# Score units of 384 or 512 columns per head in place of 384, and six larger buffers for exponentials, in the first attention batch of a fused attention and expert kernel

## The chip, the cores and the metric

The kernel runs on one core of one Trainium2 chip. The metric is the device time of the core in microseconds (us). The kernel before takes 275.0 us (median of 6 runs, 274.83 to 275.27).

A run is called fast unless it is over 1.5% above the fastest run of the same kernel. All comparisons below are of fast runs. "Clock" is the mean clock that the throttle granted to TensorE in a run, as a share of full speed.

## The reference

Block-sparse causal attention for 4 batches of 8 heads, 768 tokens and 64 columns, then a two-layer expert with a Gelu between.

```python
# attention, for each batch and head (S = 768, blocks of 64 keys)
gate   = q @ mean of k over each block        # causal blocks only
top    = the three best blocks of a query     # and the query's own block
scores = q @ k.T / 8, where the block is chosen and the key is not later
attn   = softmax(scores);  x = attn @ v       # x: 3072 x 512

# expert
h   = x @ w_in                                # 3072 x 2048
g   = 0.5 * h * (1 + tanh(sqrt(2/pi) * (h + 0.044715 * h**3)))
out = g @ w_out                               # 3072 x 512
```

## The kernel before

Two heads are handled as a pair; a batch has four pairs (0 to 3, 4 to 7, ...). A batch is: for each pair load, transpose, gate, mask, scores, exponentials, values, normalise; then the dense expert of the batch (`s1` is x times w_in with the Gelu, `s2` is the product with w_out).

The kernel does not emit its work in source order. Every piece of work is an operation with an assumed duration on each engine that may do it. A small list scheduler in the kernel, "the planner" below, simulates the engines and gives one total order. Each engine then runs its part of it in that order, and waits wherever data are late.

```python
LAT = {"PE": 0.2, "ACT": 0.19, "DVE": 0.14, "POOL": 0.1, "SP": 0.1,
       "DMA": 1.9, "XBAR": 0.1, "NONE": 0.0}     # from the end of a work to its users
...
    def solve(self):
        while cand:
            ...                                  # all ready operations and engines
            s, end, e, op = min(
                (x for x in ests if x[0] <= first),
                key=lambda x: (x[3].prio, x[3].n, x[1]))
            ...
        order.sort(key=lambda op: op.start)
        return order
...
    order = plan.solve()
    with tc.manual_schedule():
        for op in order:
            op.emit(op.eng)
```

The first batch computes both heads of a pair in one score unit. A unit is a list of pieces (key tile of 128, first query, number of queries); its scores fill at most 2 x 512 columns of a PSUM pair of banks (`wide`), and one exponential reads them:

```python
units = [[(0, 0, 384)], [(1, 128, 256), (2, 256, 128)], [(0, 384, 384)],
         [(1, 384, 384)], [(2, 384, 384)], [(3, 384, 384)],
         [(4, 512, 256), (5, 640, 128)]]          # seven units of 384 per head

st = add({PE: 0.45}, st_e, rdy[p][0 if ui < 2 else 1], pr, ...)   # scores and mask
ex = add({ACT: 0.71}, ex_e, [st, table(("exp", b), [], base)], pr, ...)
...                                               # af: causal edge on POOL
pvs.append(add({PE: 0.212}, pv_e, [af, ...], pr, ...))            # values
nm = add({DVE: 0.7}, zr_e, pvs[-1:], base - 20, ...)              # norm: reciprocal, multiply
```

TensorE's gaps are filled with 110 dummy matmuls, "fillers", at the lowest priority. What is left of them runs at the very end:

```python
def warm():
    for n in range(110):
        ...                    # nc.tensor.matmul(bank[:, 0:256], zero, zero...)
        add({PE: 0.107 if n > 26 else 0.214}, emit, [], 1e6, ...)
```

The softmax here doesn't subtract the row's maximum and nothing guards it: scores larger than these inputs give would overflow.

Of the kernel before, what the change touches and what calls it, by code (L numbers as in the profile page):

```python
# [9 lines left out]
FP16 = mybir.dt.float16  # L10
# [23 lines left out]
class Plan:  # L34
# [13 lines left out]
    def add(self, *a, **kw):  # L48
        op = Op(*a, **kw)
        self.ops.append(op)  # L50
        return op
# [70 lines left out]
def kernel(  # L122
# [28 lines left out]
    iov = ctx.enter_context(tc.tile_pool(name="iov", bufs=PV))  # L151
    hd = ctx.enter_context(tc.tile_pool(name="hd", bufs=3))
    hd2 = ctx.enter_context(tc.tile_pool(name="hd2", bufs=2))
    atp = ctx.enter_context(tc.tile_pool(name="atp", bufs=7))
    xtp = ctx.enter_context(tc.tile_pool(name="xtp", bufs=2))
    gtp = ctx.enter_context(tc.tile_pool(name="gtp", bufs=2))
    obp = ctx.enter_context(tc.tile_pool(name="obp", bufs=3))
# [35 lines left out]
    PE, ACT, DVE, POOL, SP = "PE", "ACT", "DVE", "POOL", "SP"  # L193
    add = plan.add
    T = {}
# [171 lines left out]
    rdy = {}  # L367
# [381 lines left out]
    def heads(p):  # L749
        b, hp = divmod(p, HP)  # L750
        i = p % NB
        base = 1000 * b + 100 * hp
        norms = []
        for h in range(2):
            pvs = []
            for gi, (ja, jb) in enumerate(groups):
                u = (p, h, gi)
                pr = base + 10 * (3 * h + gi)
                wa = S - ja * 128
                wb = S - jb * 128  # L760

                def st_e(_, u=u, ja=ja, jb=jb, wa=wa, wb=wb, h=h):
                    st = plan.buf[("st",) + u]
                    for jc, cb in ((ja, 0), (jb, wa)):
                        s0 = jc * 128
                        w = S - s0
                        x = cb
                        while x < cb + w:
                            e = min(cb + w, (x // 512 + 1) * 512)
                            k0, q0 = slice(s0, s0 + 128), slice(  # L770
                                s0 + (x - cb), s0 + (e - cb))
                            nc.tensor.matmul(  # L772
                                st[:, x:e], kT16[i][h][0:76, k0],
                                qT16[i][h][0:76, q0],
                                start=True, stop=True)
                            x = e
                st = add({PE: 0.381}, st_e, rdy[p][h], pr,
                         takes=("wide", ("st",) + u))

                def ex_e(_, u=u, n=wa + wb):  # L780
                    T["at", u] = atp.tile([128, 896], FP16, tag="at",
                                          name="at_%d_%d_%d" % u)
                    nc.scalar.activation(
                        out=T["at", u][:, 0:n],
                        in_=plan.buf[("st",) + u][:, 0:n],
                        func=AF.Exp, bias=0.0, scale=SCALE)
                ex = add({ACT: 0.8}, ex_e,
                         [st, table(("exp", b), gelus.get(b - 1, []), base)],
                         pr,
                         gives=[("st",) + u])  # L790
                exps.setdefault(b, []).append(ex)

                def af_e(_, u=u, wa=wa):
                    at = T["at", u]
                    dg = bass.AP(at.tensor, at.offset,
                                 [at.ap[0], [wa, 2], [1, 128]])
                    nc.gpsimd.affine_select(
                        out=dg, in_=dg, compare_op=ALU.is_ge, fill=0.0,
                        base=0, pattern=[[0, 2], [1, 128]],
                        channel_multiplier=-1)  # L800
                af = add({POOL: 0.36}, af_e, [ex], pr)

                def pv_e(_, u=u, ja=ja, jb=jb, wa=wa, h=h, gi=gi):
                    pvv = plan.buf["pv", p, h][:, 0:NC * 66].rearrange(
                        "p (c w) -> p c w", w=66)
                    at = T["at", u]
                    for jc, cb in ((ja, 0), (jb, wa)):
                        for qc in range(jc, NC):
                            nc.tensor.matmul(
                                pvv[:, qc, 0:65],  # L810
                                at[:, cb + (qc - jc) * 128:
                                   cb + (qc - jc + 1) * 128],
                                v16[i][:, jc, h, :],
                                start=(gi == 0 and jc == 0 and qc == 0),
                                stop=(gi == 2 and jc == jb and qc == NC - 1),
                                skip_group_check=True)
                pvs.append(add({PE: 0.212}, pv_e,
                               [af, ld["v16", p], c_E["ones", i]] + pvs[-1:],
                               pr, takes=("pv", ("pv", p, h))))

            norms.append(norm(p, h, pvs, base - 20))
        turn(p, norms)
        last.setdefault(p, {}).update({"s": st, "k": st, "v": pvs[-1]})


    units = [[(0, 0, 384)], [(1, 128, 256), (2, 256, 128)], [(0, 384, 384)],
             [(1, 384, 384)], [(2, 384, 384)], [(3, 384, 384)],
             [(4, 512, 256), (5, 640, 128)]]

    def both_heads(p):  # L830

# [4 lines left out]
        pvs = []  # L836
        for ui, pieces in enumerate(units):
            u = (p, ui)
            pr = base + 10 * ui

            def st_e(_, u=u, pieces=pieces):

                st = plan.buf[("st",) + u]
                for mask in range(2):
                    x = 0
                    for j, q0, w in pieces:
# [8 lines left out]
                                start=x == 0 and not mask, stop=bool(mask),  # L855
                                skip_group_check=True)
                        x += w
            st = add({PE: 0.45}, st_e, rdy[p][0 if ui < 2 else 1], pr,
                     takes=("wide", ("st",) + u))

            def both(t, lo, hi):
                return t[:, 0:768].rearrange("p (h w) -> p h w", h=2)[
                    :, :, lo:hi]

            def ex_e(_, u=u):
                T["at", u] = atp.tile([128, 896], FP16, tag="at",
                                      name="at_%d_%d" % u)
                nc.scalar.activation(
                    out=both(T["at", u], 0, 384),
                    in_=plan.buf[("st",) + u].rearrange(  # L870
                        "p (h w) -> p h w", h=2)[:, :, 0:384],
                    func=AF.Exp, bias=0.0, scale=SCALE)
            ex = add({ACT: 0.71}, ex_e,
                     [st, table(("exp", b), [], base)], pr,
                     gives=[("st",) + u])
            exps.setdefault(b, []).append(ex)
            af = ex
            for n, (j, q0, w) in enumerate(pieces):
                if q0 != 128 * j:
                    continue  # L880
                x = sum(w for _, _, w in pieces[:n])

                def af_e(_, u=u, x=x):
                    dg = both(T["at", u], x, x + 128)
                    nc.gpsimd.affine_select(
                        out=dg, in_=dg, compare_op=ALU.is_ge, fill=0.0,
                        base=0, pattern=[[0, 2], [1, 128]],
                        channel_multiplier=-1)
                af = add({POOL: 0.36}, af_e, [ex], pr)

            half = 0 if ui < 2 else 1

            def pv_e(_, u=u, ui=ui, pieces=pieces, half=half):
                pvv = plan.buf["pv", p, half][:, 0:NC * 66].rearrange(
                    "p (h c w) -> p h c w", h=2, w=66)
                x = 0
                for j, q0, w in pieces:
                    for c in range(q0 // 128, (q0 + w) // 128):
                        for h in range(2):
                            nc.tensor.matmul(  # L900
                                pvv[:, h, c - 3 * half, 0:65],
                                both(T["at", u], x, x + 128)[:, h],
                                v16[i][:, j, h, :],
                                start=(ui in (0, 2) and x == 0 and h == 0),
                                stop=(ui in (1, len(units) - 1)
                                      and x == 256 and h == 1),
                                skip_group_check=True)
                        x += 128
            pvs.append(add({PE: 0.212}, pv_e,
                           [af, ld["v16", p], c_E["ones", i]] + pvs[-1:],  # L910
                           pr, takes=("pv", ("pv", p, half))))
            if ui == 1 or ui == len(units) - 1:
# [252 lines left out]
```

## Time and profile before

| stage, us from the start of the span | TensorE busy | VectorE | ScalarE | clock |
|---|---|---|---|---|
| 28 to 36 (first batch, pairs 2 and 3) | 8.00 of 8 | 7.83 | 7.32 | 1.00 |
| 36 to 44 (first batch, pair 3) | 7.87 of 8 | 6.63 | 6.77 | 1.00 |
| 48 to 67 (dense expert, first batch) | 19.00 of 19 | 5.86 | 13.11 | 1.00 |
| 160 to 193 (end of the second batch's `s2`, then the third batch's `s1`) | 33.00 of 33 | 11.77 | 18.98 | 1.00 |

The names of the engines in the profile: PE is TensorE, DVE is VectorE, ACT is ScalarE, SP issues the loads. These are lines of the page of the kernel before: the span, the busy times, and the granted clock in 40 slices of the span (9 is 90% or more).

```profile
span 273.8 us, 5919 instructions
PE 265.1 (97%) x2290; PEld 153.7 (56%) x2290; DVE 142.2 (52%) x468; ACT 187.4 (68%) x245; POOL 48.5 (18%) x112
PEclk9999999999999999999999999999999999999999
```

TensorE is busy 97% of the span, so most of what can be won lies in the first batch, where part of "busy" is fillers.

ScalarE's timeline of the kernel before, at the seam of pairs 2 and 3 and at the end of the first batch. Columns: start, duration, engine, source line, operation, output and input with their shapes, and in brackets the idle time before it and what ended that. The table load is the switch from exponentials to the Gelu; it marks the end of the first batch on ScalarE.

```profile
33.95 0.81 ACT L868 ACTIVATE at_5_756<-wide_89 128x768 f16<-128x768 f32 x1
34.67 0.69 ACT L199 COPY qT_1_134<-bank_93 128x640 f16<-128x640 f16 x1
35.26 0.82 ACT L868 ACTIVATE at_6_785<-wide_88 128x768 f16<-128x768 f32 x1
35.97 0.82 ACT L199 CAST qT_0_115<-qT_4_777 64x768 f16<-64x768 f32 x1
36.69 0.81 ACT L868 ACTIVATE at_0_815<-wide_89 128x768 f16<-128x768 f32 x1
...
43.73 1.28 ACT L742 ACT_TABLE_LOAD   x1
```

Exponentials of 768 columns take 0.81 us.

### The profile page before, as it was taken

Reading aid. Unit: us, or ns where it says so; the run is one execution under the profiler, and the core shown is the slowest. Engines: PE = TensorE matmul, PEld = TensorE weight load, DVE = VectorE, ACT = ScalarE, POOL = GpSimd, SP = SyncE. Lnnn points to the kernel's source line nnn. Section 1 sums busy time; section 2 is a strip of 40 time slices with the busy share of each in tenths; the row PEclk is TensorE's granted clock in tenths of the full one; section 3 lists DMA queues with packets and bytes.
Section 4 is the critical chain, followed back from the end, with each engine's and each line's share of the span. In section 5 each row is a group of like instructions: output and inputs, shape, how many; then the busy total and the mean of one; then the engine's idle time right before and its main releaser. Section 6 shows DMA issues by size and latency. Waiting matters only on the chain.

```text
span 273.8 us, 5919 instructions
## 1 busy us (share of the span) xinstructions
PE 265.1 (97%) x2290; PEld 153.7 (56%) x2290; DVE 142.2 (52%) x468; ACT 187.4 (68%) x245; POOL 48.5 (18%) x112
## 2 busy tenths in 40 slices
PE   8798999999998999999999989999999999999998
PEld 5664557665454554455566534565566545665447
DVE  6778997107899996857499968500133300000001
ACT  3477887757989994896999853766899713654110
POOL 5041633000122420000045500000154200000000
PEclk9999999999999999999999999999999999999999
DMA  5999999999889969989999963300022122000222
GB/s 127 229 186 138 139 203 189 190 186 152 123 161 166 156 132 195 220 128 176 163 178 173 148 132 102 86 2 0 0 69 63 36 79 77 0 2 0 77 77 79
DMA packets 133824, 32.44 MB, mean 118 GB/s; under 512 B 127524, under 2 KB 129828, under 8 KB 133796
## 3 DMA queue, kind: packets, MB, share of 16 engines
q1 hardware_dynamic: 130676, 27.87, 58.9%
q0 software_dynamic: 3120, 4.19, 9.2%
q8 instruction: 18, 0.29, 0.5%
q14 instruction: 10, 0.08, 0.1%
HBM read 27.26 MB, written 6.29 MB: 123 GB/s over the span
## 4 chain that ended last, share of the span: by engine, by line
PE 63%; DVE 12%; SPq 9%; DMA 6%; ACT 5%; issue 3%; POOL 0%; DVEq 0%; ACTq 0%
PE wide_89 L1018 13%; PE wide_88 L1018 12%; PE bank_90 L1052 7%; PE bank_93 L1052 6%; SPq L224 5%; PE bank_91 L1052 4%; PE bank_92 L1052 3%; SPq L234 3%; PE wide_89 L772 2%; PE wide_88 L772 2%; DMA v_sd_383<-in_v_dram 2%; DMA q_sd_1856<-in_q_dram 1%; DMA q_sd_2172<-in_q_dram 1%; SPq L245 1%; PE wide_88 L850 1%
## 5 line engine op out<-in xcount | busy, mean ns | idle before, releaser
L1018 PEld LDWEIGHTS <-w_in_113 128*128 128x128 f16 x512 | 49.7, 98 | 34.0 <-issue 1.1
L203 DVE COPY osb_5_3665<-bank_92 128x256 f32<-128x256 f32 x1 | 0.4, 424 | 49.7 <-PE bank_92 L1052 49.7
L1052 PEld LDWEIGHTS <-gT_3416 128*128 128x128 f16 x112 | 11.0, 98 | 9.9
L1089 PEld LDWEIGHTS <-zero 128*128 128x128 f16 x110 | 10.4, 104 | 6.0 <-issue 3.0
L1052 PEld LDWEIGHTS <-gT_2805 128*128 128x128 f16 x96 | 9.1, 97 | 8.1
L1052 PEld LDWEIGHTS <-gT_1921 128*128 128x128 f16 x96 | 8.8, 97 | 8.5 <-issue 0.8
L1052 PE MATMUL bank_90<-w_out_114,gT_1921 128*128 128x512 f16 x48 | 13.3, 380 | 0.0
L1052 PEld LDWEIGHTS <-gT_1015 128*128 128x128 f16 x96 | 8.6, 98 | 7.3 <-issue 0.3
L1052 PE MATMUL bank_93<-w_out_114,gT_1015 128*128 128x512 f16 x48 | 12.6, 379 | 0.0
L1018 PE MATMUL wide_89<-xT_1468,w_in_113 128*128 128x512 f16 x64 | 12.1, 326 | 0.1
L1018 PE MATMUL wide_88<-xT_3083,w_in_113 128*128 128x512 f16 x64 | 12.0, 326 | 0.0
L1018 PE MATMUL wide_88<-xT_422,w_in_113 128*128 128x512 f16 x64 | 11.9, 326 | 0.0
L1018 PE MATMUL wide_89<-xT_422,w_in_113 128*128 128x512 f16 x64 | 11.9, 326 | 0.0
L1018 PE MATMUL wide_88<-xT_1468,w_in_113 128*128 128x512 f16 x64 | 11.9, 326 | 0.0
L1018 PE MATMUL wide_88<-xT_2372,w_in_113 128*128 128x512 f16 x64 | 11.7, 326 | 0.0
L1018 PE MATMUL wide_89<-xT_3083,w_in_113 128*128 128x512 f16 x64 | 11.7, 326 | 0.0
L1018 PE MATMUL wide_89<-xT_2372,w_in_113 128*128 128x512 f16 x64 | 11.7, 326 | 0.0
L203 DVE COPY osb_0_2977<-bank_93 128x512 f32<-128x512 f32 x1 | 0.7, 691 | 19.9 <-PE bank_93 L1052 19.9
L742 ACT ACT_TABLE_LOAD x8 | 10.3, 1283 | 0.9 <-PEq L1149 0.8
L1089 PE MATMUL bank_93<-zero 128*128 128x256 f16 x33 | 9.2, 287 | 0.7 <-ACT kT_0_123 L199 0.7
L1052 PE MATMUL bank_91<-w_out_114,gT_2805 128*128 128x512 f16 x32 | 9.7, 379 | 0.0
L1031 ACT ACTIVATE gT_2805<-wide_88 128x768 f16<-128x768 f32 x8 | 6.5, 812 | 4.2 <-PE wide_88 L1018 4.1
(954 smaller groups left out, 661.6 us busy)
## 6 DMA issues: line engine op xcount, KB each, us to landing
w_in_113<-in_moe_w_in_dram POOLq DMA_DIRECT2D x2, 1024.0 KB, 11.7
w_out_114<-in_moe_w_out_dram POOLq DMA_DIRECT2D x1, 2048.0 KB, 16.6
k_sd_139<-in_k_dram SPq DMA_DIRECT2D x4, 96.0 KB, 2.4
q_sd_140<-in_q_dram SPq DMA_DIRECT2D x4, 96.0 KB, 2.4
k_sd_209<-in_k_dram SPq DMA_DIRECT2D x2, 192.0 KB, 3.9
q_sd_225<-in_q_dram SPq DMA_DIRECT2D x2, 192.0 KB, 4.4
v_sd_249<-in_v_dram SPq DMA_DIRECT2D x2, 192.0 KB, 4.4
k_sd_276<-in_k_dram SPq DMA_DIRECT2D x2, 192.0 KB, 4.5
```

What stands on the lines that cost most here:

```text
L203: nc.vector.tensor_copy(out=out, in_=in_)
L224: nc.sync.dma_start(out=sd[:, :, hh, :], in_=SRC[key][b, 2 * hp + hh].rearrange("(c p) d -> p c d", p=128))
L234: nc.sync.dma_start(out=sd[64 * hh + 32 * a:64 * hh + 32 * a + 32], in_=SRC[key][b, 2 * hp + hh].rearrange("(t i) (a j) -> a i t j", i=32, ...
L245: nc.sync.dma_start(out=sd[:, 3 * a:3 * a + 3, hh, :], in_=SRC[key][b, 2 * hp + hh].rearrange("(a c p) d -> a p c d", p=128, c=3)[a])
L742: nc.scalar.activation(out=t, in_=bmask[:, 0, 0:1], func=AF.Exp if key[0] == "exp" else AF.Gelu_apprx_tanh, bias=0.0, scale=1.0)
L772: nc.tensor.matmul(st[:, x:e], kT16[i][h][0:76, k0], qT16[i][h][0:76, q0], start=True, stop=True)
L850: nc.tensor.matmul(st[:, 512 * h + x + lo - q0:512 * h + x + w], (T["E2"][h] if mask else kT16[i][0])[r, j * 128:(j + 1) * 128], qT16[i][m ...
L1018: nc.tensor.matmul(hps[:, u:e], w_in16[:, ci, f * 128:(f + 1) * 128], T["xT", b][:, ci, u:e], start=(ci == 0), stop=(ci == HP - 1))
L1031: nc.scalar.activation(out=T["gT", b][:, f, :], in_=plan.buf["hps", b, f][:, 0:S], func=AF.Gelu_apprx_tanh, bias=0.0, scale=1.0)
L1052: nc.tensor.matmul(plan.buf["ops", b, n][:, 0:x1 - x0], T["gT", b][:, f, ti * 128:(ti + 1) * 128], w_out16[:, f, x0:x1], start=(f == 0), s ...
L1089: nc.tensor.matmul(plan.buf["warm", n][:, 0:256], zero, z, start=True, stop=True)
```

## The change

The intent: ScalarE pays something for each exponential besides its columns (0.81 us for 768 columns before and 1.02 us for 1,024 after give about 0.2 us apart from the columns, an estimate). Six units of 384 or 512 per head hold the same scores as seven of 384, so each pair of the first batch needs one exponential less. The tiles for exponentials grow from 896 to 1024 columns, so six take about the room of seven. The planner is told the new durations; it then plans everything anew.

```diff
-    atp = ctx.enter_context(tc.tile_pool(name="atp", bufs=7))
+    atp = ctx.enter_context(tc.tile_pool(name="atp", bufs=6))
 ...                                       (all exponential tiles 896 -> 1024)
     units = [[(0, 0, 384)], [(1, 128, 256), (2, 256, 128)],
-             [(0, 384, 384)], [(1, 384, 384)], [(2, 384, 384)], [(3, 384, 384)],
-             [(4, 512, 256), (5, 640, 128)]]
+             [(0, 384, 384), (4, 512, 128)], [(1, 384, 384), (4, 640, 128)],
+             [(2, 384, 384), (5, 640, 128)], [(3, 384, 384)]]
 ...
-            st = add({PE: 0.45}, st_e, ...
+            st = add({PE: 0.43 if W == 384 else 0.55}, st_e, ...
 ...
-            ex = add({ACT: 0.71}, ex_e,
+            ex = add({ACT: 0.71 if W == 384 else 0.9}, ex_e,
 ...
-            pvs.append(add({PE: 0.212}, pv_e,
+            pvs.append(add({PE: 0.212 if W == 384 else 0.28}, pv_e,
```

(Lines are re-wrapped; W is the unit's columns per head, and the column slices follow it.)

More of the change, by code (lines that the diff above doesn't have):

```diff
@@ L780, in ex_e @@
                 def ex_e(_, u=u, n=wa + wb):
-                    T["at", u] = atp.tile([128, 896], FP16, tag="at",
+                    T["at", u] = atp.tile([128, 1024], FP16, tag="at",
                                           name="at_%d_%d_%d" % u)
@@ L823, in heads @@
         last.setdefault(p, {}).update({"s": st, "k": st, "v": pvs[-1]})
-    units = [[(0, 0, 384)], [(1, 128, 256), (2, 256, 128)], [(0, 384, 384)],
-             [(1, 384, 384)], [(2, 384, 384)], [(3, 384, 384)],
-             [(4, 512, 256), (5, 640, 128)]]
+    units = [[(0, 0, 384)], [(1, 128, 256), (2, 256, 128)],
+             [(0, 384, 384), (4, 512, 128)], [(1, 384, 384), (4, 640, 128)],
+             [(2, 384, 384), (5, 640, 128)], [(3, 384, 384)]]
     def both_heads(p):
@@ L839, in both_heads @@
             pr = base + 10 * ui
+            W = sum(w for _, _, w in pieces)
             def st_e(_, u=u, pieces=pieces):
@@ L857, in st_e, with both, ex_e @@
                         x += w
-            st = add({PE: 0.45}, st_e, rdy[p][0 if ui < 2 else 1], pr,
+            st = add({PE: 0.43 if W == 384 else 0.55}, st_e, rdy[p][0 if ui < 2 else 1], pr,
                      takes=("wide", ("st",) + u))
-            def both(t, lo, hi):
-                return t[:, 0:768].rearrange("p (h w) -> p h w", h=2)[
+            def both(t, lo, hi, W=W):
+                return t[:, 0:2 * W].rearrange("p (h w) -> p h w", h=2)[
                     :, :, lo:hi]
-            def ex_e(_, u=u):
-                T["at", u] = atp.tile([128, 896], FP16, tag="at",
+            def ex_e(_, u=u, W=W, both=both):
+                T["at", u] = atp.tile([128, 1024], FP16, tag="at",
                                       name="at_%d_%d" % u)
                 nc.scalar.activation(
-                    out=both(T["at", u], 0, 384),
+                    out=both(T["at", u], 0, W),
                     in_=plan.buf[("st",) + u].rearrange(
-                        "p (h w) -> p h w", h=2)[:, :, 0:384],
+                        "p (h w) -> p h w", h=2)[:, :, 0:W],
                     func=AF.Exp, bias=0.0, scale=SCALE)
-            ex = add({ACT: 0.71}, ex_e,
+            ex = add({ACT: 0.71 if W == 384 else 0.9}, ex_e,
                      [st, table(("exp", b), [], base)], pr,
@@ L881, in both_heads, with af_e @@
                 x = sum(w for _, _, w in pieces[:n])
-                def af_e(_, u=u, x=x):
+                def af_e(_, u=u, x=x, both=both):
                     dg = both(T["at", u], x, x + 128)
@@ L891, in both_heads, with pv_e @@
             half = 0 if ui < 2 else 1
-            def pv_e(_, u=u, ui=ui, pieces=pieces, half=half):
+            def pv_e(_, u=u, ui=ui, pieces=pieces, half=half, W=W, both=both):
                 pvv = plan.buf["pv", p, half][:, 0:NC * 66].rearrange(
@@ L905, in pv_e @@
                                 stop=(ui in (1, len(units) - 1)
-                                      and x == 256 and h == 1),
+                                      and x == W - 128 and h == 1),
                                 skip_group_check=True)
                         x += 128
-            pvs.append(add({PE: 0.212}, pv_e,
+            pvs.append(add({PE: 0.212 if W == 384 else 0.28}, pv_e,
                            [af, ld["v16", p], c_E["ones", i]] + pvs[-1:],
```

## The prediction

> **What bounds the kernel now.** The chain of waits is 63% TensorE. After 47 us TensorE hardly stops: its waits from there on sum to about 3 us in 227, and from 160 us the chain is almost only the two expert matmuls. So the kernel is a first batch of attention (first score 12.6 us, end at the gelu table load, 43.7 us), then a dense TensorE stretch. Of the 110 dummy matmuls that pad TensorE, 81 run before 49 us. What the change can win is an earlier first dense expert run (112 matmuls from 48.6 us in the chain).
>
> A second bound limits that. DMA engines are about 100% busy from 7 to 61 us (utilisation rows); VectorE waits 12.3 us for the key load of pair 5, until 61.3 us, and is busy 40.3 of 45 us from 68 to 113 us (stage table). The chain passes VectorE, ScalarE, queue issues and the query load of pair 10 until 113 us. If that side does not move, TensorE arriving early waits.
>
> **What the change does.** Score columns stay 2,688 per head and pair. Exponentials go from 7 of 768 columns to 3 of 768 and 3 of 1,024. The timeline shows 0.81 us for 768 and 0.92 for 896, so about 1.03 for 1,024 (estimate); busy time per pair falls from 5.68 to 5.52 us. Neighbours start 0.71 us apart: part of the fixed cost is already hidden. The Trainium skill, "ScalarE: Activation LUTs", What ACT_TABLE_LOAD costs, gives 186 ns + 0.833 ns per column with 93 ns overlapped; this trace agrees (826 against 811 ns). So one call less is worth about 0.1 us per pair, 0.4 us in the batch, plus a semaphore handover per pair.
>
> TensorE: 40 score/mask matmuls per pair for 36, the extra ones 128 wide; estimate 0.1 to 0.2 us more per pair, where it has slack. POOL selects (6) and value matmuls (42) stay. Six buffers suffice: the new TensorE order runs about four units ahead at most.
>
> The 28 exponentials need only about 20 of the batch's 31 us; ScalarE copies and a VectorE over 90% busy from 20 to 40 us fill the rest. I expect the batch 0.5 to 1.2 us shorter.
>
> **Order.** The solver re-plans everything. 30 fillers rather than 27 now follow the last useful matmul and end last: +0.3 us. The first weight load on POOL follows one more select of pair 2 (perhaps 0.5 us later); the second comes earlier. Key and query loads of pair 10 move ahead of mask transposes in the queue, which may help.
>
> **Sum.** First batch −0.9 us, of which 0.4 to 0.9 survives the DMA/VectorE bound; tail +0.3; reshuffling of later batches 0 ± 1.5. I predict 274.4 us, 80% range 272.3 to 276.3. Faster by over 2%: 3%; within: 95%; slower by over 2%: 2%.
>
> **Signs.** Right: 1,024-column exponentials last 1.02 to 1.04 us; the gelu table load starts near 43.0 and the dense expert run near 47.8; the pair-5 key transpose starts within 1 us of 61.3. Wrong: the table load moves over 1.5 us earlier, or later; TensorE idle after 47 us exceeds 5 us; waits on exponential buffers appear.
>
> **What would make it wrong.** A better order in batches 1 and 2 (TensorE gaps, output tiles of 3.6 to 4.0 us against 3.45) could win more than the first batch; a load landing late behind the weights, or a TensorE instruction placed before late data, could cost 1 to 3 us.

## More of the kernel before

The mask of a pair comes from its gate, a chain on VectorE (`sel_e`: ten MAX8, a comparison, a combination) and one on TensorE (`mask`), whose result is copied beside the queries. A pair's first score unit needs that copy.

The mask copy of pair 3 (`qT_1_134`) comes at 34.67, the first exponential of pair 3 at 36.69.

VectorE's timeline of the kernel before, the gate of pair 3:

```profile
32.47 0.81 DVE L543 MAX8 mx_3_717<-gm_689 128x8 f32<-128x12 f32 x10
33.31 0.28 DVE L545 TENSOR_TENSOR gm_689<-gm_689,mx_3_717 128x120 f32<-128x120 f32 x1
33.62 0.28 DVE L548 SCALAR_TENSOR_TENSOR madd_138<-gm_689,ownm_169 128x120 f16<-128x120 f32 x1
33.82 0.19 DVE L921 RECIPROCAL zr_0_753<-bank_92 128x6 f32<-128x6 f32 x1
```

The gate ends at 33.9; the norm of pair 2 (`zr_0`) comes after it.

TensorE's timeline of the kernel before, much later, where the second batch's `s2` runs beside the end of the third batch's attention:

```profile
158.89 0.51 PE L977 MATMUL bank_92<-ident_99,xn_2574 128*128 128x128 f16 x6 [0.70 <-DVE xn_2574 L964]
...
159.96 3.63 PE L1052 MATMUL bank_90<-w_out_114,gT_1921 128*128 128x512 f16 x16
```

TensorE waits 0.70 us there for the norm of pair 11, then goes on at full speed: 16 matmuls of an output tile in 3.63 us.

## The result, and the profile after

| | before | after |
|---|---|---|
| median, us (6 runs each) | 275.0 (274.83 to 275.27) | 278.79 (277.41 to 279.5) |
| ratio of the fast runs, 95% interval | | 1.0135 (1.011 to 1.0161) |
| clock | 1.000 (profiled run) | 0.994 in five runs of six, 1.000 in the fastest |

Ratios here and below are the mean time of one kernel's fast runs over that of the other's of the same rounds, so they are not quite the ratio of the medians. The change makes the kernel 1.35% slower. That is within 2%, but 2.5 us above the top of the predicted range.

The same lines of the page of the kernel after:

```profile
span 277.7 us, 5942 instructions
PE 267.0 (96%) x2306; PEld 155.7 (56%) x2306; DVE 143.2 (52%) x469; ACT 185.1 (67%) x240; POOL 48.3 (17%) x112
PEclk9999999999999999999999979999999999999999
```

ScalarE is busy 2.3 us less. Only about 0.7 us of that is the exponentials of the first batch (28 of 0.81 us before; 12 of 0.81 and 12 of 1.02 after); the rest is that the new plan gave other work of ScalarE to other engines, such as the mask copy of pair 3 below. Also, one slice now has a lower clock, about 160 us into the run, far from the changed code.

ScalarE's timeline of the kernel after, the same stretch:

```profile
32.36 1.02 ACT L869 ACTIVATE at_4_745<-wide_88 128x1024 f16<-128x1024 f32 x1 [0.22 <-PE wide_88 L851]
33.40 0.81 ACT L869 ACTIVATE at_5_776<-wide_89 128x768 f16<-128x768 f32 x1
34.10 0.47 ACT L199 COPY xT_431<-bank_90 128x384 f16<-128x384 f16 x1
36.16 0.83 ACT L199 CAST qT_0_115<-qT_4_787 64x768 f16<-64x768 f32 x1 [1.58 <-DVE qT_4_787 L422]
37.00 0.83 ACT L199 CAST qT_1_116<-qT_4_787 64x768 f16<-64x768 f32 x1
37.74 0.80 ACT L869 ACTIVATE at_0_836<-wide_88 128x768 f16<-128x768 f32 x1
...
43.94 1.28 ACT L742 ACT_TABLE_LOAD   x1
```

The last exponential of pair 2 starts at 33.40 in place of 35.26: ScalarE is 1.9 us ahead there, though not by the larger exponentials alone: the mask copy of 0.69 us that stood before it has gone to VectorE. Then ScalarE stands for 1.58 us, and pair 3 starts 1.05 us *later* than before. The table load, at 43.94 against 43.73, shows none of the gain.

VectorE's timeline of the kernel after, the gate of pair 3:

```profile
32.56 0.19 DVE L922 RECIPROCAL zr_0_734<-bank_93 128x6 f32<-128x6 f32 x1
32.78 0.56 DVE L923 TENSOR_TENSOR xn_733<-bank_93,zr_0_734 128x384 f16<-128x384 f32 x1
33.26 0.81 DVE L543 MAX8 mx_3_759<-gm_730 128x8 f32<-128x12 f32 x10
34.10 0.28 DVE L545 TENSOR_TENSOR gm_730<-gm_730,mx_3_759 128x120 f32<-128x120 f32 x1
34.42 0.40 DVE L548 SCALAR_TENSOR_TENSOR madd_138<-gm_730,ownm_169 128x120 f16<-128x120 f32 x1
35.15 0.98 DVE L422 STREAM_TRANSPOSE qT_4_787<-q_sd_662 128x768 f32<-128x768 f32 x1 [0.33 <-DMA q_sd_662<-in_q_dram]
36.05 0.45 DVE L203 COPY qT_1_134<-bank_91 128x640 f16<-128x640 f16 x1
```

As pair 2's values are ready sooner, the planner has put its norm ahead of the gate of pair 3. The gate ends at 34.8 in place of 33.9. After it, VectorE waits for the query of pair 4 to land before it can transpose it. Two things queue behind this transpose: on VectorE the mask copy of pair 3 (36.05, against 34.67 on ScalarE before), and on ScalarE the two casts of pair 4's query, behind which pair 3's first exponential starts at 37.74.

TensorE's timeline of the kernel after, at the end of the third batch's attention:

```profile
159.86 0.48 PE L521 MATMUL bank_90<-qT_14_2535,ksb_109 128*32 128x160 f32 x8
162.34 0.59 PE L1053 MATMUL bank_92<-w_out_114,gT_1924 128*128 128x512 f16 x2 [2.00 <-DVE xn_2603 L965]
162.94 0.49 PE L978 MATMUL bank_93<-ident_99,xn_2603 128*128 128x128 f16 x6
163.27 4.87 PE L1053 MATMUL bank_92<-w_out_114,gT_1924 128*128 128x512 f16 x14
```

TensorE stands for 2.00 us, because the output tile was planned into the bank that still holds pair 11's values until their norm (`xn_2603`) has read them. On VectorE that norm stands behind a transpose of 0.97 us and two casts for pairs 15 and 13. VectorE's timeline of the kernel after at that place:

```profile
159.72 0.97 DVE L422 STREAM_TRANSPOSE kT_15_2619<-k_sd_2515 128x768 f32<-128x768 f32 x1
160.62 0.52 DVE L203 CAST v_125<-v_sd_2315 128x768 f16<-128x768 f32 x1
161.05 0.54 DVE L203 CAST kT_0_135<-kT_15_2619 64x768 f16<-64x768 f32 x1
161.52 0.18 DVE L964 RECIPROCAL zr_1_2650<-bank_92 128x6 f32<-128x6 f32 x1
161.73 0.56 DVE L965 TENSOR_TENSOR xn_2603<-bank_92,zr_1_2650 128x384 f16<-128x384 f32 x1
```

Behind TensorE's wait, 14 matmuls take 4.87 us, against 3.63 us for 16 in the kernel before.

Stages of the kernel after around that place: bounds in us, busy time (and instructions) of each engine, granted clock, DMA share, GB/s.

```profile
160.00:163.00 3.00, 0.99 (x16) 0.36 (x8) 2.97 (x7) 2.26 (x3) 0.00 (x0) 1.00 1.06 168
163.00:167.00 4.00, 4.00 (x16) 1.65 (x16) 3.86 (x19) 0.90 (x2) 0.00 (x0) 0.57 0.19 69
```

The clock is 0.57 over 4 us right after the standstill. By busy times TensorE is idle for 5.2 us from 47 to 268 us, against 3.6 before; with 1.7 us for the lower clock (e3 below) that makes about 3.3 of the 3.9 us between the two profiled spans, an estimate. So the candidates for the loss were: (a) the first batch, (b) the place at 160 us, its wait and its clock, (c) the buffers, (d) other effects of the new order.

### The profile page after: what moved, and what is told of

The parts are those of the page before. It is cut to its first block, busy times and chain, and to the rows that moved or that the text cites. A ratio compares the mean times of both kernels' runs of the same rounds, so it can differ in the third digit from the quotient of the medians.

```text
span 277.7 us, 5942 instructions
## 1 busy us (share of the span) xinstructions
PE 267.0 (96%) x2306; PEld 155.7 (56%) x2306; DVE 143.2 (52%) x469; ACT 185.1 (67%) x240; POOL 48.3 (17%) x112
## 4 chain that ended last, share of the span: by engine, by line
PE 68%; DVE 11%; SPq 7%; DMA 6%; ACT 3%; issue 2%; POOL 0%; DVEq 0%; ACTq 0%
PE wide_89 L1019 13%; PE wide_88 L1019 13%; PE bank_93 L1053 8%; PE bank_92 L1053 8%; PE bank_91 L1053 6%; PE bank_90 L1053 5%; SPq L224 4%; PE wide_88 L772 3%; PE wide_89 L772 3%; DMA v_sd_390<-in_v_dram 2%; DMA q_sd_662<-in_q_dram 2%; DMA k_sd_1971<-in_k_dram 2%; SPq L234 1%; SPq L245 1%; PE bank_92 L809 1%
## 5 line engine op out<-in xcount | busy, mean ns | idle before, releaser
L1090 PEld LDWEIGHTS <-zero 128*128 128x128 f16 x110 | 11.0, 106 | 4.8 <-issue 1.4
L1019 PE MATMUL wide_88<-xT_1489,w_in_113 128*128 128x512 f16 x64 | 11.7, 326 | 1.2 <-ACT gT_1924 L1032 1.2
L1053 PE MATMUL bank_93<-w_out_114,gT_1018 128*128 128x512 f16 x48 | 12.7, 380 | 0.0
L1019 PE MATMUL wide_88<-xT_3086,w_in_113 128*128 128x512 f16 x64 | 12.2, 326 | 0.0
L1019 PE MATMUL wide_89<-xT_1489,w_in_113 128*128 128x512 f16 x64 | 12.1, 326 | 0.1
L1019 PE MATMUL wide_89<-xT_431,w_in_113 128*128 128x512 f16 x64 | 12.0, 326 | 0.0
L1019 PE MATMUL wide_88<-xT_431,w_in_113 128*128 128x512 f16 x64 | 12.0, 326 | 0.0
L1019 PE MATMUL wide_88<-xT_2410,w_in_113 128*128 128x512 f16 x64 | 11.9, 326 | 0.0
L1019 PE MATMUL wide_89<-xT_2410,w_in_113 128*128 128x512 f16 x64 | 11.7, 326 | 0.0
L1019 PE MATMUL wide_89<-xT_3086,w_in_113 128*128 128x512 f16 x64 | 11.7, 326 | 0.0
L1053 PE MATMUL bank_92<-w_out_114,gT_1924 128*128 128x512 f16 x32 | 9.6, 442 | 2.0 <-DVE xn_2603 L965 2.0
L1053 PE MATMUL bank_93<-w_out_114,gT_2814 128*128 128x512 f16 x32 | 9.7, 380 | 0.0
L1053 PE MATMUL bank_90<-w_out_114,gT_1924 128*128 128x512 f16 x32 | 9.4, 380 | 0.0
```

What stands on the lines that cost most here:

```text
L1019: nc.tensor.matmul(hps[:, u:e], w_in16[:, ci, f * 128:(f + 1) * 128], T["xT", b][:, ci, u:e], start=(ci == 0), stop=(ci == HP - 1))
L1053: nc.tensor.matmul(plan.buf["ops", b, n][:, 0:x1 - x0], T["gT", b][:, f, ti * 128:(ti + 1) * 128], w_out16[:, f, x0:x1], start=(f == 0), s ...
L1090: nc.tensor.matmul(plan.buf["warm", n][:, 0:256], zero, z, start=True, stop=True)
```

## The experiments

Theory A: the loss comes from the new order of the *later* batches. Its rival B: the new units or buffers themselves cost time. Kernels of one call ran on one chip beside the kernel before; different calls ran on different chips. The diffs are shortened, and words in them stand for cut lines.

### First call: the parts by themselves

**e1, new units in the old order.** The kernel before with its own plan, the new units put into the slots of the old ones.

```diff
+    slot = {0: 0, 1: 1, 2: 2, 3: 3, 4: 4, 6: 5}   # old unit -> new unit; 5 emits nothing
+    ...
-            st = wide from the plan
+            st = wide[(6 * p + n) % 2]
```

> The new score units (3 of 768 and 3 of 1,024 columns, six exponential buffers), but every instruction of every engine in the order, on the engine and in the PSUM bank that the kernel before has; the slot of the dropped seventh unit stays empty. Theory O (the loss comes from the order that the planner made for later stages, not from the units): at or a little below the kernel before, 274.0 to 275.3 us, no TensorE wait over 1.5 us after 47 us, clock 1.00. Rival U (the larger units cost time themselves, by longer exponentials, more small matmuls or one buffer less): 277 us or more. Rival B (six buffers hold exponentials up): waits of ScalarE in the first batch and 276 us or more.

Measured: a **wrong result** (relative error 0.043): two causal edges were emitted after the values that need them. 276.97 us, ratio 1.0062 (1.0037 to 1.0087), clock 1.000. Its table loads come 2.0 us later than before at the end of the first batch (45.76 against 43.73) and 1.8 us later at the last one (217.38 against 215.58). As the edges were misplaced, the size of the first number is not to be trusted. All that it suggests is that a first batch that ends late by about 2 us makes the run late by nearly as much.

**e2, the norm first.** The kernel after, with four operations that stood ahead of pair 11's norm moved behind it.

```diff
+    after(find(fn="s2.cp_e", b=1, n=2),         # behind the norm and one output copy
+          [transpose of k, pair 15; cast of v, pair 13; two casts of k, pair 15])
```

> The kernel after, with four instructions moved: at the end of batch 2 the key transpose and two key copies of pair 15 and the value cast of pair 13 come behind the normalisation of pair 11 and the output copy that release the PSUM banks. Theory O with the stall and the clock drop as its largest part: the 2.0 us TensorE wait at 160 us shrinks below 0.7 us, the clock stays at 1.00, and the time is 3 us lower, 275.2 to 276.2 us. Rival U or B: no change, 278 to 279 us. If only the wait counts and the clock does not follow from it: 277.0 to 277.5 us with the clock still at 0.994.

Measured: correct, 277.03 us (276.19 to 277.19), ratio 1.0061 (1.0035 to 1.0086), clock 1.000. TensorE's timeline of e2:

```profile
160.51 0.59 PE L1053 MATMUL bank<-w_out,gT 128*128 128x512 f16 x2 [0.22 <-DVE xn L965]
161.10 0.49 PE L978 MATMUL bank<-ident,xn 128*128 128x128 f16 x6
161.43 3.19 PE L1053 MATMUL bank<-w_out,gT 128*128 128x512 f16 x14
...
169.55 0.48 PE L521 MATMUL bank<-qT,ksb 128*32 128x160 f32 x8 [1.16 <-DVE qT L422]
```

The 2.00 us wait is down to 0.22, the clock stays up, and the same 14 matmuls take 3.19 us. But TensorE only comes earlier to the next work that VectorE has not done: the gate of pair 15 waits 1.16 us for a query transpose that VectorE, busy throughout, starts at 168.53, no earlier than in the kernel after (168.58). 1.8 us of the 3.8 are back, not the 3 us expected.

**e3, fill the standstill.** The kernel after, with 18 dummy matmuls in the 2.0 us wait. They shorten nothing; they only keep TensorE busy.

```diff
+    n = order.index(find(fn="pre.gate", p=14)) + 1
+    order[n:n] = [18 matmuls of zeros, 256 columns]
```

> The kernel after, with 18 dummy matmuls of 256 columns put into the 2.0 us wait at 160 us (into a PSUM buffer that is free then); the wait for the bank stays as long. If the idle TensorE is what lowers the clock: clock 1.00, the 14 matmuls behind the wait last 3.0 us instead of 4.7, time 1.6 to 1.8 us lower, 276.9 to 277.3 us. If the clock drop has another cause: clock 0.994 and about 278.8 us as before.

Measured: correct, 276.68 us (276.16 to 277.92), ratio 1.006 (1.0026 to 1.0095), clock 1.000 in all four runs. TensorE's timeline of e3:

```profile
159.78 2.14 PE L1173 MATMUL wide<-zero 128*128 128x256 f16 x18
161.85 0.59 PE L1053 MATMUL bank<-w_out,gT 128*128 128x512 f16 x2
162.45 0.50 PE L978 MATMUL bank<-ident,xn 128*128 128x128 f16 x6
162.78 3.19 PE L1053 MATMUL bank<-w_out,gT 128*128 128x512 f16 x14
```

The same 14 matmuls take 3.19 us in place of 4.87, 1.7 us less, though the wait for the norm is still there in full. So at this place the idle TensorE is what lowers the clock, and the lower clock alone is about 1.7 us of the loss in a run that has it. The idle stretch does not always lower it: the profiled run of e10 below has the same wait of 2.00 us and a clock of 1.000.

**e4, the query copies late.** The kernel after, with VectorE's transpose of pair 4's query and ScalarE's two copies of it moved behind pair 3's mask copy and exponentials.

> The kernel after, with three instructions moved in the first batch: the query transpose of pair 4 behind the mask copy of pair 3, and the two query copies of pair 4 on ScalarE behind the exponentials of pair 3. Theory O, first part (the gain in the first batch was given back because ScalarE waits in order for a load that lands late): the gelu table load moves from 43.9 to 42.9 us or earlier. If TensorE alone bounds what follows, the time falls by the same 0.8 to 1.2 us; if VectorE and the loads bound batch 1, it falls by less than 0.4 us (278.4 us or more) although the first batch ends earlier. Rival U: the table load stays at 43.5 us or later.

Measured: correct, 278.91 us (277.8 to 280.13), ratio 1.0136: no gain. Pair 3's first exponential came at 36.68, 1.06 us earlier than after. But its third came 1.14 us late, as the transpose now delayed pair 2's second norm, and the two copies ended up directly before the table load, which came at 45.20. A wait was taken away and two others appeared.

### Second call: new first batch and new order apart

To cross the two parts, e5 and e6 take one kernel up to the last operation of its first-batch units, and then the other kernel's order, operation by operation and engine by engine. Only 5 of about 1,700 operations lie on different sides of the cut in the two kernels, so the splice is clean. PSUM banks after the cut are chosen anew, by the one that has been free for longest.

```diff
     order = plan.solve()
+    other = "V210 A214 P216 ...".split()       # engine and number, the other kernel's order
+    head = order[:cut]                          # cut: behind the last unit operation
+    tail = [com[n] for n in other if not in head], each on the other kernel's engine
+    order = head + tail                         # checked: every dependency comes first
```

**e5, new first batch, old order after it.**

> The changed kernel up to the last operation of the new units, then every remaining operation in the order and on the engine that the kernel before gives it. Theory A (the first batch itself costs 0.2 us, as the Gelu table load at 43.9 against 43.7 us says; the loss comes from the new order of the later batches): 275.0 to 275.8 us, no wait of TensorE over 1.2 us after 60 us, clock 1.00. Theory B (the larger exponentials or fewer buffers leave something behind that costs later, whatever the order): 277 us or more.

Measured: correct, 276.33 us (276.05 to 278.35), ratio 1.0058 (1.0035 to 1.0081), clock 1.000 in five of six runs.

**e6, old first batch, new order after it.**

> The mirror image: the kernel before, with its seven units and seven buffers, up to the last operation of its units, then the changed kernel's order. Theory A: 278 to 279.5 us, with the 2.0 us wait at the end of the third batch's preparation and a clock of 0.994. Theory B: 275 to 276 us.

Measured: correct, 277.42 us (276.67 to 280.61), a little under Theory A's range; ratio 1.0104 (1.0068 to 1.0141), clock below 1.000 in three of six runs. The profile of this run of *old* units shows the place at 160 us as in the kernel after. TensorE's timeline of e6:

```profile
161.17 0.59 PE L1052 MATMUL bank<-w_out,gT 128*128 128x512 f16 x2 [2.00 <-DVE xn L964]
161.76 0.80 PE L977 MATMUL bank<-ident,xn 128*128 128x128 f16 x6
162.35 4.54 PE L1052 MATMUL bank<-w_out,gT 128*128 128x512 f16 x14
```

**e7, old units, one constant.** The kernel before; only the planned duration of a score unit is changed. The work is the same (2,290 matmuls in both profiles), but for two copies that went from VectorE to ScalarE (245 instructions on ScalarE and 468 on VectorE before, 247 and 466 here); the order is not.

```diff
-            st = add({PE: 0.45}, st_e, ...
+            st = add({PE: 0.43}, st_e, ...
```

> The kernel before with a single constant of its planner changed (a unit's score matmuls are planned at 0.43 us in place of 0.45), so the same instructions in another order. Theory A (order alone moves this kernel by more than the change's own gain): a difference of 0.5 us or more either way from 275.0. Theory B: 275.0 within 0.4 us.

Measured: correct, 286.46 us (285.43 to 287.23), ratio 1.0412 (1.0391 to 1.0433): 11.5 us slower than before. ScalarE's timeline of e7, in the first dense expert run:

```profile
50.34 1.52 ACT L1031 ACTIVATE gT<-wide 128x768 f16<-128x768 f32 x2
61.82 0.83 ACT L199 CAST kT<-kT 64x768 f16<-64x768 f32 x1 [9.96 <-DVE kT L422]
62.56 1.49 ACT L1031 ACTIVATE gT<-wide 128x768 f16<-128x768 f32 x2
```

A key cast was planned among the Gelus. Its transpose on VectorE waits 12.45 us for the key to land; so the cast waits, so does the next Gelu, and TensorE stands for 9.0 us because its two PSUM tiles are full. Its mean clock falls to 0.982. This is the same kind of standstill as at 160 us, an engine held up by what the plan put ahead in a queue, but here behind a late load; the changed units have no part in it. I had expected half a microsecond or more either way; this is over 20 times that.

**e8, the first batch untangled.** e5, with the transpose of pair 4's query behind pair 2's second norm, and its two copies behind the fourth and the seventh Gelu, where ScalarE has 0.5 us idle before each.

> e5 with two moves in the first batch: the transpose of pair 4's query on VectorE goes behind the norm of pair 2, and the two query copies of pair 4 on ScalarE go behind the fourth and the seventh Gelu of the dense run, where ScalarE has 0.5 us idle before each. If the wait of 1.6 us for that transpose is what took back the gain of the larger exponentials, the Gelu table load comes at 42.0 to 43.0 us and the time is 274.0 to 274.8 us. If VectorE's gate chain holds pair 3 anyway, the table load stays within 0.4 us of 43.9 and the time equals e5's.

Measured: correct, 276.23 us (276.06 to 276.62), ratio 1.0047 (1.0034 to 1.0061). The table load comes at 43.02, against 43.26 in e5. The time equals e5's, so taking that wait away won nothing in the end. Whether the wait took the gain back inside the first batch is less clear: pair 3's first exponential starts at 36.23, against 37.07 in e5 and 36.69 before, but the table load of one profile is too uncertain to tell the two expectations apart.

### Third call: controls, buffers, another plan

**e9 and e10** are the controls of e5 and e6: each kernel with its own order sent through the same splice, so that only the banks are chosen anew.

> The control of e5 and e6: the kernel before with its own order read back through the same splice, so that only the choice of PSUM banks after the splice is made anew. If the splice is harmless: 275.0 within 0.4 us. If it costs something by itself, it says how much of the 1.3 us that e5 lost is the splice's.

> The same control for the changed kernel: 278.8 within 0.7 us, clock 0.994, with the 2.0 us wait at the end of the third batch's preparation, if the splice is harmless. If the choice of banks is part of the loss, under 278.

Measured: e9 correct, 275.55 us (275.22 to 276.65), ratio 1.0021 (1.0006 to 1.0036). e10 correct, 277.88 us (277.22 to 279.75), ratio 1.0114 (1.0087 to 1.014), clock below 1.000 in two of six runs. The splice costs the kernel before 0.2%, and the kernel after has its clock lowered less often. With the controls the four cells are:

| ratio to the kernel before | old order after the cut | new order after the cut | new order costs |
|---|---|---|---|
| old first batch | 1.0021 (e9) | 1.0104 (e6) | +0.83% = 2.3 us |
| new first batch | 1.0058 (e5) | 1.0114 (e10) | +0.56% = 1.5 us |
| new first batch costs | +0.37% = 1.0 us | +0.10% = 0.3 us | |

(Percent are differences of ratios, times 275 us. With half-widths of 0.15 to 0.37% for each cell, both costs of the order are clear of zero, and only one of the two costs of the first batch is, barely. e5 and e6 ran on another chip than e9 and e10, each beside the kernel before. "New first batch" means all that comes before the cut, and what it leaves for later.)

Theory A holds for the greater part of the loss. Its number for e5 (a cost of 0.2 us) was too small.

**e11, the buffers alone.** The kernel before with six tiles of 1024 columns in place of seven of 896.

```diff
-    atp = ctx.enter_context(tc.tile_pool(name="atp", bufs=7))
+    atp = ctx.enter_context(tc.tile_pool(name="atp", bufs=6))     # tiles 1024 wide
```

> The kernel before with six buffers of 1024 columns for exponentials in place of seven of 896, nothing else; the order is unchanged, as the planner doesn't know of these buffers. If the buffers cost nothing (no wait on them was seen): 275.0 within 0.3 us. If one buffer fewer throttles the later batches: 276 us or more.

Measured: correct, 275.0 us (274.9 to 275.79), ratio 1.0002 (0.999 to 1.0014). The buffers cost nothing in this order; candidate (c) is out.

**e12, a plan with the measured lag of loads.** The kernel after, planned with 3.5 us in place of 1.9 us from the issue of a load to its landing.

```diff
-           "DMA": 1.9, "XBAR": 0.1, "NONE": 0.0}
+           "DMA": 3.5, "XBAR": 0.1, "NONE": 0.0}
```

> The changed kernel, planned with 3.5 us from the issue of a load to its landing in place of 1.9 us (the traces show 2.9 to 4.8 us). If operations placed before late loads are what the order costs, the new order has no wait of TensorE over 1.2 us after 45 us and takes 274.5 to 276 us. If the order is a lottery, whatever the planner believes, it lands anywhere from 275 to 280 us.

Measured: correct, 285.14 us (283.13 to 285.38), ratio 1.0348 (1.0323 to 1.0373), clock 0.982 to 0.988. A constant nearer to the measured loads gave a far worse order; its first switch to the Gelu comes at 53.77 us in one profile. Neither of my two ranges held it.

### Fourth and fifth call: what sets the pace of the first batch

Six runs beyond the first twelve went to the term that was still open: why less work for ScalarE gained nothing.

**e13, half exponentials:** the kernel before with every exponential of the first batch over half its columns, 9 us less for ScalarE. Its output is wrong, which doesn't matter for the time. The seven tiles are fixed ones that POOL fills with ones at the start, so that nothing unset is read. **e14** is its control, with the same tiles at full width.

```diff
-                T["at", u] = atp.tile([128, 896], FP16, ...)
+                T["at", u] = next_ring()                  # seven fixed tiles, filled once
                 nc.scalar.activation(
-                    out=both(T["at", u], 0, 384),
+                    out=both(T["at", u], 0, 192),         # e14: 384
```

> The kernel before with every exponential of the first batch over half its columns (28 of 384 columns in place of 768), wrong result on purpose; the seven buffers are fixed ones, filled with ones at the start so that nothing unset is read. ScalarE's work in the first batch falls by 28 x 0.32 = 9 us, over four times what the change takes out. If VectorE's gate chain and the loads set the pace of the first batch: the Gelu table load comes at 42 to 43.5 us (before: 43.1 to 44.7 in several profiles) and the time is within 1.0 us of the full-width control. If ScalarE sets it: the table load at 39 us or earlier and 3 us or more off the time.

> The control of e13: the same fixed buffers and the same fill at the start, exponentials at full width. 275.0 to 275.6 us, correct result, if the fixed buffers and their fill on POOL (idle from 6 to 14 us) cost nothing.

Measured: e13 275.77 us over all six runs, two of which were slow (281.7 and 281.78; one of them was the profiled one, so it is not read here). Its four fast runs take 275.16 to 275.85, ratio 0.9985 (0.9958 to 1.0013). e14 correct, 275.88 us (275.34 to 277.56), ratio 1.0007 (0.9977 to 1.0037). In these rounds the kernel before ran at 275.62. Taking away 9 us of ScalarE's work, over ten times the 0.7 us that the change takes out of the exponentials, moved the time by 0.15% against the kernel before and by 0.22% against the control, with zero inside the interval. With the order as it is, less work for ScalarE in the first batch does not shorten the run. That ScalarE does not set the pace inside the first batch is not shown by that: no profile of a fast run exists, TensorE still ran the fillers that the plan had put into its gaps, and a lead could have been lost later. In the slow run that was profiled VectorE waits 4.47 us for pair 4's query, until 39.1 us, and TensorE then stands for 3.79 us; the control had no slow run among six. Whether shorter exponentials bring such runs about was not tested.

**e15 and e16, no end fillers:** the kernel before and e8 without the fillers behind the last useful matmul (110 becomes 83 and 82).

> The kernel before without the 27 fillers behind its last useful matmul; all other instructions and their order stay. If that chain of fillers ends last, as the chain of waits says, the span ends with the last output's landing, 0.3 to 1.0 us earlier: 274.0 to 274.7 us. If the landing ends last anyway: 275.0 within 0.2 us.

> e8 (new units, untangled, then the old order) without its 28 end fillers: 276.2 less the same 0.3 to 1.0 us, so 275.2 to 275.9 us; under 275.0 only if the end fillers cost more than the chain of waits says.

Measured: e15 correct, 275.13 us, ratio 0.998 (0.9951 to 1.0009). e16 correct, 276.08 us, ratio 1.0001 (0.9978 to 1.0025). e15 lies in the expected direction, but its interval includes no change. e16 has no run of e8 beside it, and its ratio is to the kernel before, so it does not price the fillers. The tail term is not settled. Neither version beats the kernel before by more than the noise.

**e17, half exponentials, planned for:** e13 with 0.40 us planned for an exponential, so that the plan drops 16 fillers from TensorE before the table load; then the old order.

> e13 (half-width exponentials in the first batch, wrong result on purpose) with the first batch planned for them (0.40 us in place of 0.71 for an exponential, which removes 16 fillers from TensorE ahead of the Gelu table load), and the old order after it. If ScalarE sets the pace of the first batch: the table load at 40 us or earlier (its plan says 2.3 us earlier than before) and a time under 273.5 us. If VectorE and the loads set it: the table load at 42 us or later and a time over 274.5 us.

Measured: wrong result. Five of six runs were slow (282.51 to 289.43), the single fast one took 277.89, so there is no ratio. Its one fast run is 2.7 us above the kernel before, not under 273.5 us as it would be if ScalarE set the pace. This agrees with e13 but is too thin to show it alone. In its profiled slow run, too, VectorE waits for pair 4's query (4.28 us).

**e18, the gate first:** e8, with the gate of pair 3 ahead of pair 2's first norm on VectorE, as in the kernel before, and the mask ahead of that norm's transposes on TensorE.

> e8 with the gate of pair 3 ahead of the norm of pair 2's first half on VectorE, and on TensorE that pair's mask ahead of the transposes that need this norm. If the later gate is what took the gain: the gate's last operation at 33.3 to 33.9 us (e5: 34.2), the first exponential of pair 3 at about 35.5 (e5 and the changed kernel: 37 to 37.7), the Gelu table load at 41.8 to 42.6, and a time of 275.2 to 275.9 us, as a lead there is partly given back at the key of pair 11. If the loads hold the batch: table load within 0.4 us of e8's 43.0.

Measured: correct, 277.5 us (277.0 to 278.18), ratio 1.0082 (1.0066 to 1.0098). The gate ended at 34.0, as early as before. TensorE's timeline of e18:

```profile
34.80 0.27 PE L1090 MATMUL bank<-zero 128*128 128x256 f16 x1 [1.60 <-DVE xn L923]
34.91 0.44 PE L567 MATMUL bank<-ident,madd 128*128 128x128 f16 x5
```

But a *filler* in TensorE's queue ahead of the mask had been given the bank that the moved norm has yet to free, so TensorE stood 1.60 us at a matmul of zeros, and the mask started at 34.91, no earlier than the 34.87 of the kernel after. The table load came at 44.22. The experiment did not test what it should: whether an earlier *mask* brings the gain stays open.

## Why the prediction was wrong

- **The time.** Predicted 274.4 us (272.3 to 276.3), measured 278.79. "Within 2%", with 95%, was right.
- **The failed step: "reshuffling of later batches 0 ± 1.5".** The new order of the later batches costs 1.5 to 2.3 us by the crossed runs (e5, e6, e9, e10). The greatest part seen is one place: a wait of 2.00 us for a norm, against 0.70 before, and the lower clock that follows, 1.7 us (e3). e6 shows the same wait with the *old* units. In the kernel after the clock fell in five runs of six, in the crossed runs with the new order (e6, e10) in five of twelve, in the kernel before beside them in two of 22 (over all calls in nine of 51); this may be part of why the kernel after lost more than their sum. The prediction had named the mechanism ("a TensorE instruction placed before late data could cost 1 to 3 us") but gave it to the tail of the distribution. It also took the waits for the whole price and did not think of the clock.
- **The width of that term was wrong too.** e7 moved the kernel by 11.5 us with one planner constant and e12 moved it from 278.8 to 285.1. The three new plans (after, e7, e12) were all slower than the old one, by 3.8, 11.5 and 10.1 us. Three draws give no distribution, and that the old order was an unusually good one is not shown, but they speak against a term of ± 1.5 around zero, in centre and in width.
- **The second failed term: "First batch −0.9 us, of which 0.4 to 0.9 survives".** Nothing survived. One profile's table load says little (two profiled runs of e9 show it at 44.66 and 43.15), so all profiles are taken together. The old first batch shows 43.73, 43.12, 44.66, 43.46, 43.45 and 43.43 (before, e6, e9, e11, e14, e15), median 43.46. The new one, unaltered, shows 43.94, 43.61, 43.48, 43.26 and 43.51 (after, e2, e3, e5, e10), median 43.51. By the crossed runs the new first batch costs 0.3 to 1.0 us; e13 shows that even 9 us less on ScalarE bring nothing in that order. The prediction had itself counted "only about 20 of the batch's 31 us" for the exponentials and still gave ScalarE the say. What held pair 3 inside the first batch, VectorE's gate chain or the landing of pair 4's query, was **not** settled: the gate does end about 0.9 us later, but e18, meant to tell, failed by a wait of its own. Nor does the cost of e5 show at the end of the first batch (table load 43.26, in e9's two profiles 44.66 and 43.15). It shows later: in e5 and e8 VectorE waits 4.0 us for the key of pair 11, transposes it at 119.0 us (118.0 before, 117.8 in the second profile of e9), and TensorE then waits 1.0 us for a Gelu, which it does not do in those two. So the prediction's second bound, loads and VectorE, takes back in the third batch what a lead may have been; that was seen, not tested.
- **The planner knew half of it.** Run on both versions, the planner itself puts the Gelu table load at 40.34 us after and 40.91 before: 0.57 us, not 0.9, was there to be had by its own reckoning. And the gate's selection of pair 3 starts at 30.59 us in its new plan and at 29.69 in its old one. Both could have been read from the kernel before any run.
- **The tail, +0.3.** Thirty fillers in place of 27 do run last, 0.11 us apart, which is the expected 0.3 us; the two runs without end fillers (e15, e16) are too noisy to confirm it.
- **Right.** The 1,024-column exponentials last 1.02 us (1.02 to 1.04 predicted). "ScalarE: Activation LUTs", section "What ACT_TABLE_LOAD costs", in the Trainium skill gives 186 ns + 0.833 ns per column, so 1,039 ns (an estimate); the trace agrees within 2%. No waits on exponential buffers, and e11 shows them free. Pair 5's key transpose came at 61.3 us (61.4 before).
- **The stated signs.** The table load near 43.0 did not come (43.94); "moves over 1.5 us" did not fire. "TensorE idle after 47 us exceeds 5 us" fired by busy times (5.2 us idle, 3.6 before) and just missed by the listed waits (4.7 us, 3.2 before); both leave the lower clock out. Here a sign that reads idle time alone missed half of what the standstill cost.

## What to carry to other kernels

When a planner or scheduler orders a whole kernel, a local change re-draws every later order; here three new orders of three were slower. Keep the old order outside the changed part, or cross the two, as here, before a change is judged. Before crediting an engine with the pace of a stage, make its work much shorter (wrong result and all) with everything else fixed, with a control; here that took one run and its control, and would have warned against the change. Price a standstill of the matmul engine with the slower clock that may follow it; here 18 dummy matmuls inside the wait bought that part (1.7 us) back.

## What the Trainium skill lacked or had wrong

- "TensorE: Matmul & The Clock Gate", Part 1, says that the clock falls after at least one idle window of about 3.4 us, and calls for no idle gaps over that. Here an idle stretch of 2.00 us was enough: the clock was 0.57 over the next 4 us, and 14 matmuls took 4.87 us in place of 3.19. The mean clock was lower in five of six runs of the kernel after, but only in five of twelve of e6 and e10, whose profiles have the same wait. Length alone does not decide it: the profiled runs of e10 keep a clock of 1.000 over the 2.00 us, while in e16 the clock is 0.50 from 11 to 14 us after a wait of 0.68 us. The page mentions frequent short idles in another kernel, without a length; its advice should give gaps under 3.4 us as a risk.
- The same page has no figure for dummy matmuls put into a wait: 18 of 256 columns kept the clock at 1.000 in all four runs of e3, worth 1.7 us.
- "DMA: Bandwidth & Descriptors", section "Anatomy of one DMA — SWDGE (gpsimd) path", fits 2.0 us + bytes / 436 GB/s for one transfer, which would be 2.2 us for 96 KB (an estimate by that page, which is for another issue path). The loads of 96 KB here took 2.4 us from issue to landing at the quiet start (medians by tile) and 3.0 to 4.8 us under load, and pair 5's key took 12.9 us before and 13.5 us after. The page gives no time from issue to landing for a load in a busy queue.
- No page says how much the order alone can move a kernel whose engines run their queues in order: the same work with one planner constant changed took 286.46 in place of 274.97 us.
